# Turning batch 2's plain probabilities by transposing DMAs in a fused windowed-attention and MLP kernel

## The chip, the cores and the metric

The kernel runs on one core of a Trainium2 chip. The metric is the device time of one execution in microseconds (us), the median of several. Engines are named as in the profile: PE (TensorE), DVE (VectorE), ACT (ScalarE), POOL (GpSimd) and SP (SyncE, which here only issues DMAs).

## The reference

Eight batches of attention with 8 heads, 576 positions and 64 features per head, each followed by one layer pair of an MLP. Heads 0 to 3 see a plain window of 32 positions back; heads 4 to 7 see every fourth position of a window of 128 (a *strided* window).

```python
scores = scale * np.matmul(q, k.transpose(0, 1, 3, 2))
mask_plain = (rel >= 0) & (rel < window)                     # window = 32
mask_dil = (rel >= 0) & (rel < window * dilation) & (rel % dilation == 0)   # dilation = 4
...
attn = np.exp(scores - max)
attn = attn / (np.sum(attn, axis=-1, keepdims=True) + 1e-09)
attn_out = np.matmul(attn, v)
...
x = attn_out.transpose(0, 2, 1, 3).reshape(B * S, H * D)     # 4608 x 512
h = x @ w_in                                                 # w_in 512 x 2048
out = (h * (1.0 / (1.0 + np.exp(-h)))) @ w_out               # w_out 2048 x 512
```

## The kernel before

**Attention of one batch** is done in two halves, `z = 0` (the plain heads) and `z = 1` (the strided heads), and each half in two groups, `hi = 0` and `hi = 1`. Since only a window is seen, scores are small tiles: 32 queries by 64 keys, four of them stacked on 128 partitions. A group holds 8 or 10 such columns of 64 keys (`width`): from batch 1 on the plain half's first group has 8, so 512 elements per partition, and the three others have 10, so 640. The steps of a half are functions:

- `scores`: small matmuls on PE (L379 for `z = 0`, L391 for `z = 1`) into PSUM tiles of pool `ps`; DVE scales, masks and takes maxima (L512, L521, L528);
- `exps`: exponentials on ACT (L551 in one instruction where the maxima were already subtracted, else L560, one for each column of keys, with the sums taken along);
- `normal`: DVE divides by the sum and writes `pn` in float16 (L569 where sums are still missing, L573, L574, L576);
- the turning of `pn`, so that keys lie on partitions, into `ptT`. There are two forms. `turn` and `turned`: PE transposes 128x128 blocks, 4 or 5 for a group, into a PSUM tile of pool `ps` (L585), and a copy brings them to SBUF (L593). `turn_by_dma`: one transposing DMA from SBUF to SBUF, issued from SP (L600);
- `values`: 64 small matmuls (L627) and the rows left over (L691) into four PSUM tiles of pool `ps`;
- `finish`: four casts (L704, and L696 or L698) into `xT`, the input of the MLP.

**The MLP of one batch** is `layer1` (16 blocks, PE L717, then Silu on ACT, L725) and `layer2` (PE L782, 16 matmuls of 512 columns for a tile of 128 rows; even batches do tiles 0 to 3 of a pair of batches, odd ones tiles 4 to 8). `store` copies a tile to SBUF (L766, pool `o32` with five buffers) and issues its store from SP (L767).

**The order is written out by hand.** Instructions run on each engine in program order. While the MLP of batch `b` is issued, `plan_of(b)` puts steps of the attention of batches `b+1` and `b+2` between its pieces. `at(s, fn, ...)` puts a call at step `s`: steps 0 to 15 stand before the blocks of `layer1`, and from 16 on a step stands before each four matmuls of `layer2`, so an odd batch has steps 16 to 35. What stands at one step is issued in the order of the `at` calls. The change is in the plan of `b == 1`, in which batch 2's attention is finished and batch 3's plain scores are made.

**DMAs.** Loads are issued from POOL (`load_rows`, L134 and L141, `load_v`, L177 to L190), with a cast from float32 to float16. SP issues the stores, the transposing DMAs of whole batches of q and k (`cross`, L152 for the plain half, L158 and L159 for the strided one), and `turn_by_dma`. SP waits for the semaphores of a DMA before it issues it, and so holds up those behind it. In the plan of `b == 1` the loads of batch 4 are issued from step 17 on, batch 3's `cross` stands at step 2 and batch 4's at step 28.

**PSUM.** Pool `ps` has four tiles, pool `big` (for both layers) two. Scores of a half take three tiles of `ps`, a pair of `turn` two, `values` four.

In the plan of `b == 1`, both plain groups are normalised at step 19 and turned by PE at step 27, with their value products at step 28; the strided groups are normalised at steps 29 and 31, turned at 33, and have their products at 34. Batches 4 to 7, and the strided half of batch 3, are turned by `turn_by_dma`.

Of the kernel before, what the change touches and what calls it, by code (L numbers as in the profile page):

```python
# [29 lines left out]
def kernel(  # L30
# [764 lines left out]
    def transposes(at, b, z, step):  # L795
        for which in (1, 0):
            at(step, transpose, b, z, which, both)

    def later(at, b, z, steps, copies=(nc.vector.tensor_copy, nc.vector.tensor_copy)):

        for hi in (0, 1):
            if steps[hi] is not None:
                at(steps[hi], normal, b, z, hi)
        for hi in (0, 1):
            at(steps[2], turn, b, z, hi)
        for hi in (0, 1):
            at(steps[2], turned, b, z, hi, copies[hi])
        at(steps[3], values, b, z)
        at(steps[3], finish, b, z, copies)

    def plan_of(b):
        ev = {}

        def at(s, fn, *args):
            ev.setdefault(s, []).append((fn, args))

        def all_exps(b, z):
            for hi in (0, 1):
                at(16, exps, b, z, hi)

        if b == 0:

            at(-16, normal, 0, 1, 1)
            at(-15, shift_class, 0, dve, 1, 2)
            at(-14, normal, 0, 0, 1)
            at(-8, turn, 0, 1, 1)
            at(-8, turned, 0, 1, 1, act)
            at(-4, turn, 0, 0, 1)
            at(-4, turned, 0, 0, 1)
            at(-4, values0, 1, 1)  # L830
            at(-4, last_values, 0, 1, (1,))
            at(-4, finish0, 1, 1)
            at(-4, last_finish, 0, 1, 1)
            at(-2, values0, 0, 1)
            at(-2, last_values, 0, 0, (1,))
            at(-2, finish0, 0, 1, both)
            at(-2, last_finish, 0, 0, 1)
            at(-2, clear_short, 1, nc.vector)
            at(-2, load_v, 1)
            for c in (2, 3):  # L840
                at(-2, load_w_out, c)
            at(-2, load_qk, 2)
            transposes(at, 1, 1, 2)
            at(8, scores, 1, 1)
            for hi in (0, 1):
                at(8, shift, 1, 1, hi)
            for which in (1, 0):
                at(18, transpose, 1, 0, which, (dve, dve) if which else (act, act))
            at(20, normal, 1, 1, 0)
            at(20, scores, 1, 0)  # L850
            at(14, shift_v, 1, nc.sync.dma_start)
            at(18, load_rows, 3)
            at(18, load_v, 2)
            all_exps(1, 1)
            for hi in (0, 1):
                at(20, exps, 1, 0, hi)
            for n, z, hi in ((20, 1, 1), (26, 0, 0), (28, 0, 1)):
                at(n, normal, 1, z, hi)
            for n, z, copies in ((27, 1, (dve, dve)), (30, 0, both)):
                for hi in (0, 1):  # L860
                    at(n, turn, 1, z, hi)
                for hi in (0, 1):
                    at(n, turned, 1, z, hi, copies[hi])
                at(n + 1 + z, values, 1, z)
                at(n + 1 + z, finish, 1, z, both)
        elif b == 1:
            transposes(at, 2, 0, 3)
            transposes(at, 2, 1, 11)
            at(2, shift_v, 2, nc.sync.dma_start)
            for z in (0, 1):  # L870
                at(2, cross, 3, z)
                at(28, cross, 4, z)
            at(9, scores, 2, 0)
            for hi in (0, 1):
                at(12, shift, 2, 0, hi)
            at(17, load_v, 3)
            at(17, nc.gpsimd.tensor_copy, latch, qTs[1][:, 1, S - 1 : S])
            at(17, load_rows, 4)
            at(14, scores, 2, 1)
            all_exps(2, 0)  # L880
            all_exps(2, 1)
            for hi in (0, 1):
                at(19, normal, 2, 0, hi)
            at(21, scores, 3, 0)
            at(21, exps, 3, 0, 0)
            at(21, exps, 3, 0, 1)
            later(at, 2, 0, (None, None, 27, 28))
            later(at, 2, 1, (29, 31, 33, 34))
        else:
            if b + 2 < B:  # L890
                at(0, load_v, b + 2)
                if b + 3 < B:
                    at(0, load_rows, b + 3, (1, 0))
                if b + 3 < B:
                    at(12, cross, b + 3, 0)
                if b > 2:
                    at(12, cross, b + 2, 1)
            if b + 1 < B:
                at(1 if b == 2 else 0, shift_plain, b + 1, dve, 0, NM)
                at(12, shift_class, b + 1, dve, 0, 2)  # L900
                at(12, shift_over, b + 1, dve)
                if b == 2:
                    later(at, 3, 0, (0, 0, 4, 6))
                else:
                    at(6, values, b + 1, 0)
                    at(6, finish, b + 1, 0)
                x = {2: 13, 3: 12}.get(b, 11)
                at(x, scores, b + 1, 1)
                at(x, shift, b + 1, 1, 1)
                all_exps(b + 1, 1)  # L910
            if b + 2 < B:
                at(18 if b == 2 else 17, scores, b + 2, 0)
                for hi in (0, 1):
                    at(18, exps, b + 2, 0, hi)
            if b + 1 < B:
                for hi in (0, 1):
                    at(22 + hi, normal, b + 1, 1, hi)
                    at(22 + hi, turn_by_dma, b + 1, 1, hi)
                at(29, values, b + 1, 1)
                at(29, finish, b + 1, 1)  # L920
            if b + 2 < B:
                for hi in (0, 1):
                    at(27 + hi, normal, b + 2, 0, hi)
                    at(27 + hi, turn_by_dma, b + 2, 0, hi)

        def plan(s):
            for fn, args in ev.pop(s, ()):
                fn(*args)

        return plan  # L930
# [49 lines left out]
    for b in range(B):  # L980
        plan = plan_of(b)
        if b == 0:
            for x in range(NFF):
                plan(2 * x - NFF)
                plan(2 * x + 1 - NFF)
                layer1_part(2 * x % NFF, 2 * x // NFF, first[x] if x < 4 else None)
        else:
            for f in range(NFF):
                plan(f)
                layer1(b, f)  # L990
        if b == 0:
            layer2_first(plan)
        else:
            layer2(b, plan)
        for s in range(NFF, 3 * NFF):
            plan(s)
# [30 lines left out]
```

## Time and profile before

| | |
|---|---|
| three runs | 308.22, 307.44, 308.28 us; median 308.22 |
| the profiled execution | 307.98 us, of which the span from first to last instruction is 306.1 |
| PE | busy 294.8 us, 96% of the span; mean granted clock 0.989 |
| DVE, ACT, POOL | busy 178.2, 187.5 and 92.3 us |
| DMA, software queue (issued from POOL) | 18.88 MB in 63104 packets |
| DMA, hardware queue (issued from SP) | 19.60 MB in 41584 packets |

The profile is of one execution. The span has 40 slices of 7.65 us in the page's second part, with the busy share of each engine in tenths. "The chain" is the work that ended last, followed back from the last instruction to what released it. In a timeline a row has a start, a duration, the engine, the line, the operation, what it writes and reads, and a count; DMA rows of SP and POOL give the time of the issue, and the landing is told apart from it.

### The profile page before, as it was taken

What the parts mean: (1) busy time and instruction counts of PE and PEld (TensorE: products, weight loads), DVE (VectorE), ACT (ScalarE), POOL (GpSimd) and SP (SyncE); (2) the same over time, 40 slices, a digit from 0 to 9 for tenths busy, and PEclk for the clock granted to TensorE, in tenths of its full rate; (3) what the DMA queues carried; (4) which work ended last, traced back from release to release, by engine and by line L of the source; (5) the groups of instructions that cost most, each with busy time, mean ns of one, the idle gap of its engine ahead of it and who ended that gap; (6) DMA issues with size and microseconds to landing.
All of it is one profiled execution on the core that took longest, in us unless ns stands there. A gap on an engine that the chain in (4) does not pass through costs nothing.

```text
span 306.1 us, 10365 instructions
## 1 busy us (share of the span) xinstructions
PE 294.8 (96%) x4466; PEld 189.2 (62%) x4466; DVE 178.2 (58%) x370; ACT 187.5 (61%) x556; POOL 92.3 (30%) x139
## 2 busy tenths in 40 slices
PE   5689999999999999999999999999999999999995
PEld 2557754677555875477644775467644775477544
DVE  6896579518797738943785447842885344620011
ACT  2676677676894559945792558945793558246200
POOL 8634544962473831086007610040000000000000
PEclk9689999999999999999999999999999999999999
DMA  8999999999999999599889995494035000400022
GB/s 106 179 213 203 174 197 218 170 197 182 164 156 191 170 189 103 135 141 176 108 154 176 194 113 105 130 177 82 4 77 144 36 2 12 135 36 2 9 94 71
DMA packets 104878, 39.21 MB, mean 128 GB/s; under 512 B 79568, under 2 KB 100048, under 8 KB 104832
## 3 DMA queue, kind: packets, MB, share of 16 engines
q0 software_dynamic: 63104, 18.88, 62.6%
q1 hardware_dynamic: 41584, 19.60, 30.3%
q8 instruction: 35, 0.57, 0.8%
q14 instruction: 11, 0.09, 0.1%
q10 hardware_dynamic: 144, 0.07, 0.1%
HBM read 37.75 MB, written 9.44 MB: 154 GB/s over the span
## 4 chain that ended last, share of the span: by engine, by line
PE 87%; DMA 7%; ACT 2%; DVE 1%; issue 1%; POOL 1%; POOLq 0%; SPq 0%
PE h L717 36%; PE o L782 33%; PE o L756 5%; PE h L737 4%; DMA w_in<-in_moe_w_in_dram 4%; PE x L627 3%; DMA nat<-in_q_dram 2%; PE s L379 1%; PE s L391 1%; ACT pe L560 1%; PE t L329 1%; PE pt L585 1%; DMA ptT<-pn 1%; POOL nat L168 1%; PE xs L691 1%
## 5 line engine op out<-in xcount | busy, mean ns | idle before, releaser
L725 ACT ACTIVATE gT<-h 128x576 f16<-128x576 f32 x112 | 72.9, 651 | 77.5 <-PE h L717 77.3
L782 PE MATMUL o<-w_out,gT 128*128 128x512 f16 (+1 forms) x528 | 114.1, 373 | 0.0
L717 PE MATMUL h<-xT,w_in 128*128 128x288 f16 x896 | 113.5, 286 | 0.0
L717 PEld LDWEIGHTS <-w_in 128*128 128x128 f16 x896 | 86.4, 98 | 23.3 <-DVE xT L704 0.3
L782 PEld LDWEIGHTS <-gT 128*128 128x128 f16 x528 | 50.7, 98 | 54.9
L560 ACT ACTIVATE pe<-ms,nm 128x64 f32<-128x64 f32 x178 | 59.1, 333 | 2.8 <-DVE nm L528 2.7
L766 DVE COPY ob<-o 128x512 f32<-128x512 f32 (+1 forms) x34 | 23.1, 681 | 45.9 <-PE o L782 44.9
L512 DVE SCALAR_TENSOR_TENSOR ms<-s,mask 128x512 f32<-128x512 f32 x28 | 19.2, 686 | 35.7 <-PE s L391 24.7
L560 ACT ACTIVATION_READ_ACCUMULATOR pe<-ms,nm 128x1 f32 x178 | 33.2, 187 | 0.0
L704 DVE CAST xT<-x 128x512 f16<-128x512 f32 x26 | 16.8, 685 | 21.2 <-PE xs L691 21.2
L177 POOL DMA_DIRECT2D vw<-in_v_dram x16 | 10.1, 634 | 61.4 <-PE xs L691 59.2
L576 DVE TENSOR_TENSOR pn<-pe,r 128x640 f16<-128x640 f32 (+2 forms) x32 | 25.3, 792 | 1.1
L528 DVE TENSOR_REDUCE nm<-ms 128x10 f32<-128x640 f32 (+1 forms) x28 | 22.0, 787 | 1.0
L737 PE MATMUL h<-xT,w_in 128*128 128x256 f16 (+1 forms) x128 | 16.9, 286 | 1.6 <-issue 0.9
L134 POOL DMA_DIRECT2D nat<-in_k_dram x20 | 15.2, 764 | 6.7 <-DMA vw<-in_v_dram 6.0
L134 POOL DMA_DIRECT2D nat<-in_q_dram x20 | 14.6, 749 | 6.3 <-DMA nat<-in_k_dram 4.0
L756 PE MATMUL o<-w_out,gT 128*128 128x512 f16 x64 | 15.2, 379 | 0.2 <-issue 0.2
L737 PEld LDWEIGHTS <-w_in 128*128 128x128 f16 x128 | 11.9, 98 | 5.4 <-issue 1.9
L744 ACT ACTIVATE gT<-h 128x512 f16<-128x512 f32 (+1 forms) x16 | 10.1, 652 | 6.3 <-PE h L737 6.1
L627 PEld LDWEIGHTS <-vw 64*64 64x64 f16 x896 | 8.4, 108 | 5.2 <-issue 5.2
L766 ACT COPY ob_last<-o 128x128 f32<-128x128 f32 x1 | 0.3, 266 | 17.0 <-DVE ob_last L766 17.0
L569 DVE TENSOR_REDUCE l<-pe 128x10 f32<-128x640 f32 (+2 forms) x12 | 9.6, 801 | 1.5 <-ACT pe L551 1.4
(101 smaller groups left out, 257.7 us busy)
## 6 DMA issues: line engine op xcount, KB each, us to landing
out_dram<-ob SPq DMA_DIRECT2D x35, 256.0 KB, 2.5
vw<-in_v_dram POOLq DMA_DIRECT2D x8, 288.0 KB, 8.4
vw<-in_v_dram POOLq DMA_DIRECT2D x16, 128.0 KB, 5.6
w_in<-in_moe_w_in_dram POOLq DMA_DIRECT2D x4, 512.0 KB, 12.5
w_out<-in_moe_w_out_dram POOLq DMA_DIRECT2D x4, 512.0 KB, 11.2
nat<-in_k_dram POOLq DMA_DIRECT2D x6, 256.0 KB, 6.8
nat<-in_q_dram POOLq DMA_DIRECT2D x6, 256.0 KB, 8.2
nat<-in_k_dram POOLq DMA_DIRECT2D x20, 72.0 KB, 7.1
```

The lines of the kernel that those rows point to most:

```text
L134: nc.gpsimd.dma_start(out=f[:, 2 * (1 - which) + h // 2, 0 : ZR - 1, h % 2], in_=src[b, h].rearrange("(m p) d -> p m d", p=RT),)
L512: nc.vector.scalar_tensor_tensor(out=ms[:, 0:8].rearrange("p (n t) c -> p n (t c)", n=2), in0=s[hi].rearrange("p n t c -> p n (t c)"), sca ...
L528: nc.vector.tensor_reduce(out=nm[:, 0:w], in_=ms[:, 0:w], axis=AX.X, op=ALU.max, negate=True)
L560: nc.scalar.activation(pe[:, t, :], slot(t), AF.Exp, scale=1.0 if b else scale, bias=nm[:, t : t + 1], accum_out=l[:, t : t + 1],)
L576: nc.vector.tensor_tensor(pn[:, 0:w], a["pe", z, hi][:, 0:w], r[:, 0:w, None].broadcast_to([P, w, KB]), ALU.mult)
L627: nc.tensor.matmul(dst, w, p, start=True, stop=True)
L717: nc.tensor.matmul(h[:, half, 0:HS], w_in16[:, c, f * P : f * P + P], xT[:, c, half * HS : half * HS + HS], start=(c == 0), stop=(c == MC ...
L725: nc.scalar.activation(gT[:, f, s0 : s0 + S].rearrange("p (a c) -> p a c", a=2), h[:, :, 0:HS], AF.Silu)
L737: nc.tensor.matmul(h[:, i, 0 : c1 - c0], w_in16[:, c, (f + i) * P : (f + i + 1) * P], xT[:, c, c0:c1], start=(c == 0), stop=(c == MC - 1),)
L756: nc.tensor.matmul(o, gT[:, f, t * P : (t + 1) * P], w_out16[:, f, :], start=(f == 0), stop=(f == NFF - 1),)
L766: copy(ob, o)
L782: nc.tensor.matmul(o, gT[:, f, t * P : (t + 1) * P], w_out16[:, f, m0:m1], start=(f == 0), stop=(f == NFF - 1),)
```

## The change

For batch 2's plain half, in the plan of `b == 1`:

- each group is turned by a transposing DMA, issued from SP right behind its `normal` at step 19, in the place of nine PE transposes and two DVE copies at step 27;
- `values` and `finish` go from step 28 to step 30;
- the strided half's second `normal` goes from step 31 to step 29, beside the first, so that both now stand ahead of the plain half's `finish` in DVE's order.

`later` loses a condition that only this batch used.

```diff
     def later(at, b, z, steps, copies=(nc.vector.tensor_copy, nc.vector.tensor_copy)):
 
         for hi in (0, 1):
-            if steps[hi] is not None:
-                at(steps[hi], normal, b, z, hi)
+            at(steps[hi], normal, b, z, hi)
         for hi in (0, 1):
             at(steps[2], turn, b, z, hi)
         for hi in (0, 1):
...
             for hi in (0, 1):
                 at(19, normal, 2, 0, hi)
+                at(19, turn_by_dma, 2, 0, hi)
             at(21, scores, 3, 0)
             at(21, exps, 3, 0, 0)
             at(21, exps, 3, 0, 1)
-            later(at, 2, 0, (None, None, 27, 28))
-            later(at, 2, 1, (29, 31, 33, 34))
+            at(30, values, 2, 0)
+            at(30, finish, 2, 0)
+            later(at, 2, 1, (29, 29, 33, 34))
```

## The prediction

> **What bounds the kernel now.** I read the page's shares and slices first, then the chain of waits around batch 1's second layer, then the timelines of DVE, SP and POOL there, and last the DMAs by line.
>
> ```profile
> PE 294.8 (96%) x4466; PEld 189.2 (62%) x4466; DVE 178.2 (58%) x370; ACT 187.5 (61%) x556; POOL 92.3 (30%) x139
> PE   5689999999999999999999999999999999999995
> DMA  8999999999999999599889995494035000400022
> PE 87%; DMA 7%; ACT 2%; DVE 1%; issue 1%; POOL 1%; POOLq 0%; SPq 0%
> ```
>
> PE is full in every slice but the first few. So what leaves PE's stream comes off the end, and what PE has to wait for is added to it. The DMA engines are almost as full through 24 slices (184 us), one excepted, and batch 1's second layer (78 to 99 us, slices 11 to 13) lies in that. The chain of waits there is PE alone:
>
> ```profile
> 82.41 0.61 PE s L379 x64
> 83.02 0.08 PE ss L379 x6
> 83.10 5.29 PE o L782 x24
> 88.39 0.50 PE pt L585 x9
> 88.89 0.86 PE o L782 x4
> 89.75 0.61 PE x L627 x64
> 90.37 0.06 PE xs L691 x8
> 90.43 4.42 PE o L782 x20
> 94.85 0.56 PE pt L585 x10
> 95.41 0.86 PE o L782 x4
> ```
>
> A step of the plan is four matmuls, 0.86 us. Scores of batch 3 are step 21 (82.41), the turning of batch 2's plain pair step 27 (88.39), its value products step 28 (89.75), the strided pair's turning step 33 (94.85). No gap: PE waits for nothing here. DVE (start, us, line):
>
> ```profile
> 81.92 0.69 DVE L576 TENSOR_TENSOR pn<-pe,r 128x512 f16<-128x512 f32 x1
> 83.85 0.82 DVE L576 TENSOR_TENSOR pn<-pe,r 128x640 f16<-128x640 f32 x1
> 88.76 0.81 DVE L593 COPY ptT<-pt 128x512 f16<-128x512 f16 x2
> ```
>
> The two plain groups' `pn` are ready at 82.6 and 84.7. PE turns them 3.7 us after the second. SP's and POOL's DMAs:
>
> ```profile
> 77.35 3.86 SPq L158 DMA_TRANSPOSE strided<-nat  x1
> 81.31 2.14 SPq L159 DMA_TRANSPOSE strided<-nat  x1
> 85.31 5.53 SPq L767 DMA_DIRECT2D out_dram<-ob  x3
> 81.36 2.94 POOL L134 DMA_DIRECT2D nat<-in_k_dram  x4
> 84.26 2.96 POOL L134 DMA_DIRECT2D nat<-in_q_dram  x4
> L600 SPq DMA_TRANSPOSE ptT<-pn x18: 1199/1208/2481, 124.0 to 263.8; - x18
> DMA to landing us min/median/max: 2.4/2.6/7.9
> ```
>
> SP has issued its last transposition for batch 3 at 83.45 and idles until the store at 85.31. POOL issues batch 4's row loads from 81.36 on. The last two lines are the turnings by DMA of the later batches: 1.2 us of issue, landing 2.6 us in the median and 7.9 at worst.
>
> **The sum is made against the profiled execution**, 307.98 us (span 306.1 and 1.9 around it); the median of the three runs is 308.22, within their spread of 0.84.
>
> **Removed from PE.** Nine 128x128 transposes, 4 for the narrow group and 5 for the wide one: 0.50 us in the chain, 55 ns each. Both neighbours are matmuls at their usual pace (0.86 us for four before and after), so all 0.50 us goes. One instruction lasts 219 ns by its row, but they overlap.
>
> [...]
>
> **Removed from DVE.** Two copies PSUM to SBUF, 0.81 us in all. I cost this at nothing: PE is at matmuls meanwhile, and the only PE work behind them was step 28, which moves.
>
> **Added to SP and the DMA engines.** Two transposing DMAs, ahead of the store of tile 4. The first needs `pn` (82.6) and SP (83.45): issue at about 83.5. It takes 1.2 to 2.5 us to issue, and the second `pn` is ready at 84.7, so the second issues at 84.8 to 86.0. Behind them SP holds the stores of tiles 4, 5 and 6 and batch 4's four transpositions. The first store goes from 85.31 to 86.0 to 87.2, the others (88.87 and 90.5) hardly move. There are five store buffers, and the next tile to want tile 4's is in the following layer, at about 120 us: no one waits. Batch 4's transpositions (91.07) wait for loads; they are read by its scores at 118.44, some 17 us after they land, so a microsecond of contention is covered. If it were not, PE would wait at 118 for the excess.
>
> **Value products, moved from step 28 to step 30.** Without the turning, step 28 starts at 88.39 + 0.86 = 89.25 and step 30 at 90.97, say 91.0. That is the due time of the second DMA. Its landing is the one unknown cost. Best: 2.6 us after issue, 87.4 to 88.6, no wait. Worst: 7.9 (the turning issued at 130.12, with loads queued at the same moment), 92.7 to 93.9, a wait of 1.7 to 2.9 us. Nearest in place are the DMAs on both sides of it on the same queue: the small transposition issued at 81.31 landed after 4.7 us (2.6 for its like at 155.03, with no loads in flight), the store at 85.31 after 2.7 us, only 0.2 over the median of the stores. I take 4.3 us for a transposition between them: landing at 89.1 to 90.3, before 91.0 by 0.7 to 1.9 us. No wait, but no great margin.
>
> **DVE's order.** Both normalisings of the strided pair (2.4 us, 91.89 to 94.28 before) now stand between tile 6's copy and the plain pair's `finish`. Tile 6's copy ends at 89.9, the normalisings at 92.3 (their exponentials are done at 87.9). The products are done at 91.65, so the four casts wait 0.65 us on DVE and end at 93.8; tile 7's copy follows, done by 94.5. Who waits for that: the strided pair's turning at step 33 (now 94.35) wants the PSUM banks that the casts free at 92.9 and 93.6. Cover: 0.8 us. If it is gone, each microsecond is PE's. The two strided copies start at about 94.67, when tile 7's copy is just done, as close as before. The last casts into `xT` end at 98.0 and the next layer starts at 98.4. DVE's total falls, so I cost the reorder at nothing. From both sides: a gain is excluded because PE has no idle time there to win; a loss is at most the 0.65 us of DVE wait.
>
> **Sum.** 307.98 - 0.50 = 307.48, so 307.5 us, 0.16% less. About 0.3% (0.92 us) is what a measurement of this kernel can tell from no change; so the forecast is a small gain inside that.
>
> **Rivals.**
>
> *The second DMA lands late, and PE waits at step 30.* For it: the POOL rows above, eight loads of small packets in the same microseconds; four of the later turnings that met loads landed after 7.9, 5.6, 5.8 and 3.3 us; and SP's own 2.14 us for a transposition that elsewhere issues in 1.2. Against: the store at 85.31 passed almost freely. The change breaks even at a landing of 91.5 and is slower by over 0.92 us from 92.4. With issue at 85.5 and 7.9 us it lands at 93.4: a wait of 2.4 us, net 1.9, 309.9 us. Chance of over 0.92 us: 0.20. A landing between 91.5 and 92.4, 308.0 to 308.9: another 0.08, inside "same".
>
> [...]
>
> *The 0.50 us is refilled.* PE is then held at the same place by something else: the banks at step 33, or an output tile whose copy is late behind the normalisings. For: DVE is busy 2.4 of each 2.5 us there. Against: 0.8 us of slack at step 33, and tile 7's copy ends as early as before. 308.0 us, chance 0.08.
>
> *PE gains more than the chain shows.* If the nine transposes cost PE their full 219 ns, that is 1.97 us, and 306.0. The chain's start times (88.39 to 88.89) speak against it. Chance 0.03.
>
> **The numbers.** Forecast (no wait, or one that leaves a gain) 0.61; late by over 0.92 us 0.20; break-even or refilled 0.16; larger gain 0.03. Medians of three runs move by a few tenths of a microsecond here, so some of the forecast falls beyond 0.92 us on the faster side: 0.09 of it, with the larger gain 0.12. Slower gets 0.20 and 0.02 for the same reason from the break-even case: 0.22. The rest, 0.66, is within 0.3%. The range runs from 306.9 (the gain and a low median) to 309.2, which takes in a wait of up to 1.7 us and leaves out the worst landings.
>
> **What would show it.** Right: the chain after has no L585 between step 21 and step 33; its matmuls run on from 83.1 for nine steps to the value products at about 91.0; no idle time before L627; two L600 rows more on SP near 83.5 and 85; and the strided turning at about 94.35. Wrong: idle time of PE ahead of L627 released by the DMA `ptT<-pn`; landing of the two over 5.5 us; idle time ahead of L585 released by a cast; or scores of batch 4 that wait for `plain`.

## The result, and the profile after

The changed kernel takes 309.77 us in the median of 11 runs (308.72 to 313.23); the kernel before, run as often, 308.22 (307.44 to 309.47). The ratio is 1.0053, with a 95% interval of 1.0029 to 1.0078. So it is slower by half a per cent, where a gain of 0.16% was forecast, and outside the range. The spread has grown too. Medians here and below are of all runs; the ratios leave out runs over 1.5% above the fastest of the same kernel, of which `same_again` and `turn_first` have two each and `no_turn` one. The profiled execution took 308.80 us, with a span of 307.0.

The chain of waits after, in the same stretch (start, duration in us, what):

```profile
82.64 2.70 PE o L782 x12
...
85.45 5.21 DMA ptT<-pn
90.66 0.04 issue
90.70 0.68 PE x L627 x63
91.38 0.06 PE xs L691 x8
91.44 2.70 PE o L782 x12
94.14 0.56 PE pt L585 x10
94.70 0.86 PE o L782 x4
95.56 0.62 PE x L627 x62
96.18 0.91 issue
97.09 0.21 PE x L627 x2
```

The nine transposes are gone. The second turning lands at 90.66, and the first value products start at once. PE's rows have no idle time there: 36 matmuls from 82.64 take PE to about 90.5, so this wait is 0.2 us at most. The main loss is further down. PE stops for 0.91 us in the middle of the *strided* value products, after 62 of 64. "issue" means that the profile shows nothing that PE waited for. The change did not touch these products.

The two turnings, in SP's timeline and in the answer for L600 over 83 to 86 us:

```profile
83.64 3.02 SPq L600 DMA_TRANSPOSE ptT<-pn  x2
```

```profile
DMA to landing us min/median/max: 5.2/5.4/5.7
```

They are issued where they were expected and land after 5.7 and 5.2 us. As a measure for all runs below I take *the window*: from the first matmul of batch 1's second layer (L782) to the first of batch 2's first layer (L717), by PE's rows. It was 77.93 to 98.73 before, 20.80 us, and is 77.34 to 99.09 after, 21.75 us: 0.95 more in place of 0.50 less. From the start of the last product ahead of the gap to the start of the next is 1.10 us; the rest is in rows a little longer than before (scores 0.74 for 0.61, products 0.68 for 0.61) and in the small wait. Before and after this window the two profiles differ by what start-up and tail give.

### The profile page after: what moved, and what is told of

It is laid out like the page before. It is cut to its first block, busy times and chain, and to the rows that moved or that the text cites. A ratio compares the mean times of both kernels' runs of the same rounds, so it can differ in the third digit from the quotient of the medians.

```text
span 307.0 us, 10351 instructions
## 1 busy us (share of the span) xinstructions
PE 296.5 (97%) x4457; PEld 190.5 (62%) x4457; DVE 178.0 (58%) x368; ACT 187.3 (61%) x556; POOL 92.6 (30%) x139
## 4 chain that ended last, share of the span: by engine, by line
PE 90%; DMA 3%; DVE 2%; ACT 2%; issue 1%; POOL 1%; POOLq 0%; SPq 0%
PE h L717 36%; PE o L782 31%; PE h L737 5%; PE o L756 5%; PE x L627 3%; DMA ptT<-pn 3%; PE s L391 2%; PE s L379 2%; PE pt L585 1%; ACT pe L560 1%; PE t L329 1%; PE t L369 1%; PE xs L691 1%; DVE pn L576 1%; PE s L444 1%
## 5 line engine op out<-in xcount | busy, mean ns | idle before, releaser
L782 PE MATMUL o<-w_out,gT 128*128 128x512 f16 (+1 forms) x528 | 113.9, 373 | 0.0
L717 PE MATMUL h<-xT,w_in 128*128 128x288 f16 x896 | 113.5, 286 | 0.0
L717 PEld LDWEIGHTS <-w_in 128*128 128x128 f16 x896 | 86.4, 98 | 23.3 <-DVE xT L704 0.3
L782 PEld LDWEIGHTS <-gT 128*128 128x128 f16 x528 | 50.7, 98 | 55.1
L627 PEld LDWEIGHTS <-vw 64*64 64x64 f16 x896 | 8.7, 108 | 6.4 <-issue 6.2
L627 PE MATMUL x<-ptT,vw 64*64 64x32 f16 x896 | 10.5, 187 | 1.1 <-issue 0.9
```

The costliest lines, as they stand in the source:

```text
L627: nc.tensor.matmul(dst, w, p, start=True, stop=True)
L717: nc.tensor.matmul(h[:, half, 0:HS], w_in16[:, c, f * P : f * P + P], xT[:, c, half * HS : half * HS + HS], start=(c == 0), stop=(c == MC ...
L782: nc.tensor.matmul(o, gT[:, f, t * P : (t + 1) * P], w_out16[:, f, m0:m1], start=(f == 0), stop=(f == NFF - 1),)
```

## The experiments

Three theories. **Landing**: PE waits at step 30 for the second DMA. **Order**: DVE's normalisings ahead of the casts hold PE up. **Instruction supply**: PE is held by its own instructions.

The third comes from the page of the profile. Its instruction queue (q8) moved 35 packets and 0.57 MB, and in the trace's DMA packets each is 16 KB. PE has 4457 matmuls and as many weight loads, 8914 instructions. The 0.57 MB over these is about 64 bytes each, so a packet holds some 256 of them. Counted in weight loads and matmuls from the start of PE's stream, the gap stands at instruction 3516. The two gaps marked "issue" in the kernel before, at 21 and 48 us in start-up and batch 0, stand at 702 and 1724. Divided by 256 these leave 190 and 188, and 3516 leaves 188. So by estimate there is such a place every 256 instructions (all 45 such stops of 0.15 us or more in the 14 profiles leave 188 or 190); below I call it an *edge*, and the instructions between two edges a *block*. The previous edge, 3260, lies in the plain value products, which the change moved two steps closer.

### The change alone, without DMAs, without the turning by DMA, and DMAs alone

`same_again` is the changed kernel once more.

> The changed kernel as it is, profiled once more. In its first profile PE reached the value products of step 30 at 90.5 us, the second transposing DMA landed at 90.66, and the chain had 0.9 us of issue (PE waits for nothing that the profile shows) among the strided pair's value products at 96.2. Theory 1, landing: PE waits at step 30 for the second DMA, by an amount that differs from run to run; expected 309 to 311 us, and in the profile idle time of PE ahead of the first L627 of step 30 that equals landing minus about 90.5. Theory 2, instruction supply: PE is held by late instructions in the dense stretches of small matmuls; expected 309 to 310 us, with an issue gap of about 0.9 us near 96 us and none ahead of step 30. Theory 3, order: DVE's normalisings ahead of the casts hold PE at step 33; an idle time ahead of L585 at step 33.

310.30 us, ratio 1.0041 (1.0021 to 1.0061). Window 21.43, no idle time ahead of step 30, 0.97 us of issue after the same 62 products.

`no_turn` leaves out the turning of batch 2's plain pair:

```diff
-                at(19, turn_by_dma, 2, 0, hi)
+                at(19, no_turn, 2, 0, hi)      # products read a zeroed tile
```

> The changed kernel without the two transposing DMAs: batch 2's plain value products read a zeroed tile in place of the turned probabilities (that part of the computation is left out). PE's and DVE's orders are those of the changed kernel. Theory 1, landing: the wait is gone, 0.50 us under before, about 307.7 us, no gap at step 30. Theory 2, if PE's shorter stream alone moves the fetch into the dense stretch: the issue gap of 0.9 us stays, about 308.6 us; if the added DMA traffic delays the fetch: about 307.7. Theory 3, order: stays slower, 308.7 us or more.

309.42 us, ratio 1.0031 (1.0008 to 1.0054). Window 22.07, with 1.50 us of issue after 62 products. There is nothing to land and the gap is there, so the landing is not its cause.

`extra_dma` adds the two DMAs to the kernel before, with nobody waiting:

```diff
                 at(19, normal, 2, 0, hi)
+                at(19, turn_aside, 2, 0, hi)   # the same transposing DMA, into a spare tile
```

> The kernel before, with the same two transposing DMAs issued from SP at the same place (behind each plain normalising at step 19) into a spare tile that nobody reads; PE still turns the pair at step 27. Theory 1, landing: nobody waits for them, so no change, 308.2 us within 0.3. Theory 2 by added traffic: PE's instructions come late, 0.5 to 1 us slower, with an issue gap between 85 and 98 us. Theory 3, order: no change.

308.89 us, ratio 1.0019 (1.0003 to 1.0035). Window 20.80, no gap. The traffic alone costs at most little, and its profile doesn't show where.

`order_only` is the kernel before, turned by PE, with the new steps:

```diff
-            later(at, 2, 0, (None, None, 27, 28))
-            later(at, 2, 1, (29, 31, 33, 34))
+            later(at, 2, 0, (None, None, 27, 30))
+            later(at, 2, 1, (29, 29, 33, 34))
```

> The kernel before, still turned by PE at step 27, with the value products and finish of the plain pair at step 30 and both strided normalisings at step 29 ahead of them: the reorder alone. Theories 1 and 2: no change, 308.2 us within 0.3. Theory 3: slower by 0.4 us or more, with PE idle ahead of L585 at step 33 or ahead of the strided value products.

310.30 us, ratio 1.0049 (1.0025 to 1.0074): the whole loss, without the two DMAs. By the expectation above this is what the theory of order forecast, and not what instruction supply did. What speaks for supply is where the gap stands:

```profile
97.19 0.55 PE x L627 x53
97.74 1.46 issue
99.20 0.27 PE x L627 x10
```

The gap comes after 53 products, not 62. The nine transposes, which are still there, are nine weight loads and nine matmuls ahead of it. So it is the same instruction of the stream, 3516, and not the same piece of work. PE has no idle time ahead of the strided turning either, where a late cast would hold it.

### The normalisings or the distance

`values_late` moves only the plain products:

```diff
-            later(at, 2, 0, (None, None, 27, 28))
+            later(at, 2, 0, (None, None, 27, 30))
```

> The kernel before with one edit: the plain pair's value products and finish at step 30 in place of 28, still turned by PE, and the strided normalisings where they were, at 29 and 31. Theory 2, instruction supply: the two dense stretches of value products stand four steps apart in place of six, so the issue gap is there, 1 to 1.7 us among the strided value products, 309.3 to 310.5 us. Theory 3, order of the normalisings: no change, 308.4 us.

310.33 us, ratio 1.0044 (1.0017 to 1.0070), with 0.58 us of issue after 53 products, less than the 1 to 1.7 expected. The normalisings stand at the steps where they were, and the loss is there. But the casts of `finish` moved to step 30, so the first of the normalisings, at 29, now stands ahead of them on DVE. This run alone does not clear the order.

`no_turn_28` is `no_turn` with the plain products back at step 28; both normalisings stay at 29.

```diff
-            at(30, values, 2, 0)
-            at(30, finish, 2, 0)
+            at(28, values, 2, 0)
+            at(28, finish, 2, 0)
```

> The kernel without the two transposing DMAs (batch 2's plain value products read a zeroed tile, so that part of the computation is left out), with the plain value products and finish back at step 28; both strided normalisings at step 29. Theory 2, instruction supply, block edges: the edge in the plain products and the one in the strided products, 256 instructions on, are again some 6.6 us apart, as before (6.7 us, no gap). No gap or one under 0.3 us, and what PE no longer turns is gained: 0.3 to 0.5 us under before, 308.0 to 308.2 us. Theory 3, order of the normalisings: still slower, 309 us or more. If the gap depended on added DMA traffic or on the shorter stream alone, it would be here too.

307.73 us against 308.97, ratio 0.9967 (0.9953 to 0.9982), and all seven runs lie within 0.64 us. The chain runs through:

```profile
89.67 0.61 PE x L631 x64
...
90.35 4.42 PE o L786 x20
...
96.20 0.64 PE x L631 x64
96.84 0.14 PE xs L695 x16
```

(L631 and L786 are L627 and L782, four lines down.) The window is 78.35 to 98.65, 20.30 us: 0.50 under before, to the hundredth what the transposes were costed at. With the casts back at step 28 both normalisings stand behind them, as before, so these two runs together still can't tell the order from the distance. The runs below can: `pad_here` and `split_loads` keep the changed kernel's order, with both normalisings ahead of the casts, and have no gap here, and `turn_first` has the order of the kernel before and the longest gap of all. So order falls. What is left is how far apart the two dense stretches stand (the plain and the strided value products, 64 small matmuls in some 0.6 us each): six steps or four.

### Moving the edges

`shift_after` and `shift_before` put 64 tiny matmuls at the start of PE's stream, half a block:

```diff
     keep_busy(big.tile([P, 2, 512], F32, tag="big", name="busy")[:, 0], 4)
+    tiny = big.tile([P, 2, 512], F32, tag="big", name="tiny")
+    for _ in range(64):
+        nc.tensor.matmul(tiny[0:W, 0, 0:W], ident[:, 0:W], ident[:, 0:W], start=True, stop=True)
```

> The changed kernel with 64 tiny matmuls more at the start of PE's stream, where PE waits for the first loads anyway. Each has a weight load, so all later work lies 128 instructions further on in PE's stream, half a block of 256. Theory 2, instruction supply: the gap sits at a fixed instruction (after 62 strided products, after 53 where nine transposes stand ahead of them), the edge of a block; moved by half a block, the edge falls among the matmuls of 512 columns and the block that holds both dense stretches is gone: no issue gap between 90 and 98 us, 0.5 us under before, 307.8 to 308.2 us, unless an edge elsewhere becomes bad. Theories 1 and 3: no change against the changed kernel, 309.5 to 310.3 us.

> The kernel before with the same 64 tiny matmuls at the start: what the shift alone does. Theory 2: no gap in this place before and none after, 308.2 to 308.7 us, unless an edge elsewhere becomes bad, which the issue rows of the chain would show. Theories 1 and 3: no change, 308.4 us.

The totals miss: 316.83 us, ratio 1.0261 (1.0229 to 1.0293), and 313.97, ratio 1.0161 (1.0128 to 1.0194). In the window the expectation holds: 20.55 us and no gap for the changed kernel, 20.80 for the one before. But the other edges moved too. In the changed kernel shifted, PE waits elsewhere:

```profile
PE x L627 <- issue: 1.9, 1, 1.9
PE s L379 <- issue: 1.8, 1, 1.8
PE x L627 <- DMA ptT<-pn: 1.4, 1, 1.4
PE s L391 <- issue: 1.1, 1, 1.1
```

Its gaps stand at instructions 446, 702, 1212, 2236 and 3004, which leave 190, 190, 188, 188 and 188. The work in these places is the kernel's as it was. Ahead of batch 1's first layer the gaps make 5.6 us, where the changed kernel has 0.9, and this layer starts at 64.97 us in place of 58.30. So most of what the shift cost was lost at edges, before batch 2's attention came to its value products.

`pad_here` puts them into the changed kernel just ahead of the plain products:

```diff
+            at(27, tiny, 64)                   # 64 tiny matmuls into a PSUM tile that nobody reads
             at(30, values, 2, 0)
```

> The changed kernel with 64 tiny matmuls more (128 instructions) at step 27, into a PSUM tile that nobody reads: more work for PE, some 0.6 us by the rows of the 64 scores or products. Theory 2, block edges: the edges move half a block, out of the value products into the matmuls of 512 columns, so the issue gap at 96 us (0.9 to 1.7 us) goes; the profile has no gap between 88 and 99 us, and the time is near before, 308.3 to 308.9 us, less than the changed kernel's 310 in spite of the added work; later edges move too and could cost a few tenths. Theory 1 (landing) or 3 (order): the added work only adds, or fills a wait for the landing: 310 to 310.6 us.

312.15 us, ratio 1.0115 (1.0088 to 1.0141). The chain:

```profile
88.58 1.70 PE tiny L798 x64
...
97.77 0.64 PE x L627 x64
```

The gap is gone, as expected, and the window is 22.10, where 20.80 - 0.50 + 1.70 makes 22.00. But the tiny matmuls cost 1.70 us and not the 0.6 that I expected, and another 1.6 us is lost in batch 2's second layer, where PE waits 1.4 us for a turning of batch 3. So it shows the edge, not a cheaper kernel.

### The loads

`loads_later` was to keep batch 4's loads out of the stretch:

```diff
-            at(17, load_rows, 4)
+            at(31, load_rows, 4)
-                at(28, cross, 4, z)
+                at(34, cross, 4, z)
```

> The changed kernel with batch 4's row loads issued at step 31 in place of 17, and batch 4's cross at step 34 in place of 28, so that few loads are in flight between 83 and 93 us. Theory 2, instruction supply: PE's instructions come in blocks of 16 KB by DMA (the instruction queue of the page; 570 KB for 8932 instructions, 64 bytes each, so 256 in a block); a block comes late when loads fill the DMA engines and PE runs through 256 instructions quickly. With fewer loads the block comes in time: the issue gap of 0.9 to 1.7 us among the strided value products goes or shrinks, and the time is 307.8 to 308.3 us, under before. Theory 1, landing: the turning lands after 2.6 to 4 us and the time is the same 307.9. Theory 3, order: the gap and the 0.4% stay, 309.5 us or more.

311.94 us, ratio 1.0100 (1.0056 to 1.0144), and the edit did not do what it was for. A step did not tie POOL to PE: POOL issued the loads at 81.46 (81.36 in the kernel before). What moved was batch 4's cross, behind a store. The gap stayed (1.06 us), and 2.8 us were lost in batch 2's second layer, where PE met another gap and a late turning.

`split_loads` ties the strided loads (L141) to the end of batch 2's attention:

```diff
+    def gate():
+        nc.gpsimd.tensor_copy(latch, att(2)["xT"][:, HP - 1, S - 1 : S])
...
-            at(17, load_rows, 4)
+            at(17, load_rows, 4, (0,))
...
+            at(34, gate)
+            at(34, load_rows, 4, (1,))          # and batch 4's strided cross at step 35
```

> The changed kernel with batch 4's strided row loads held back until batch 2's attention is finished (POOL copies one element of the finished xT first) and batch 4's strided cross after the stores of the layer; the plain row loads stay. So few loads are in flight when PE's next block of instructions is fetched, between 91 and 97 us. Theory 2, with contention: the fetch starts 1 to 1.5 us after the block's edge in place of 3 to 4, the gap goes, and the time is 0.3 to 0.5 us under before, 308.0 to 308.3 us. Theory 2 without contention (a block simply takes 6 us): the gap stays, 309.5 to 310.3. A new wait at batch 4's strided scores near 145 us would show as PE idle ahead of L391.

313.71 us, ratio 1.0152 (1.0128 to 1.0176), where 308.0 to 308.3 were expected. In the window this worked: L141 at 99.93 in place of 87, and the strided products run through, though the edges are only 5.1 us apart.

```profile
97.08 0.64 PE x L627 x64
...
119.25 0.59 PE s L379 x61
119.83 2.06 issue
```

The window is 20.41, 0.39 under before. The loads then lie upon a later block: its packet starts 5.3 us after the edge ahead of it, PE stands still for 2.06 us at 119.83, and batch 3's turnings hold it for 2.5 us more in two waits.

### A version meant to be faster

`turn_first` issues the turnings ahead of batch 3's strided cross and keeps the six steps:

```diff
+            at(2, cross, 3, 0)
+            at(20, cross, 3, 1)
             for z in (0, 1):
-                at(2, cross, 3, z)
...
-            at(30, values, 2, 0)
-            at(30, finish, 2, 0)
-            later(at, 2, 1, (29, 29, 33, 34))
+            at(28, values, 2, 0)
+            at(28, finish, 2, 0)
+            later(at, 2, 1, (29, 31, 33, 34))
```

> A version meant to keep the 0.50 us: batch 2's plain pair turned by the two DMAs, but batch 3's strided cross (two transposing DMAs that are read only at 113 us) moved behind them in SP's order, from step 2 to step 20; plain value products and finish at step 28 and the strided normalisings at 29 and 31, as before. Theory 2, block edges: the two dense stretches are six steps apart again, so no issue gap near 96 us; the turnings are issued at about 82.7 and 84.8 with no other transposition ahead of them and land after 2.6 to 4.5 us, at 87.4 to 89.3, when PE wants them at 89.3: 0.50 us under before, 0.2 at worst if the second lands late; 308.0 to 308.4 us against 308.5 to 309.0. The moved cross is then in flight together with batch 4's loads; if that holds up the blocks of instructions, a gap near 96 or 105 us appears and the gain is gone. Theory 1, landing: a wait at step 28 ahead of L627, 1 us or more.

316.96 us, ratio 1.0239 (1.0200 to 1.0277): the worst case named, and more. SP's timeline, PE's waits for the turning, the chain, and the busy times by stretch:

```profile
87.05 5.01 SPq L158 DMA_TRANSPOSE strided<-nat  x1
```

```profile
PE x L627 <- DMA ptT<-pn: 0.8, 1, 0.8
```

```profile
96.88 0.62 PE x L627 x62
97.50 3.58 issue
...
101.41 3.37 PE o L782 x8
```

```profile
97.50:101.00 3.50, 0.00 (x1) 0.00 (x0) 0.69 (x1) 0.00 (x0) 0.62 (x1) 1.00 1.44 119
101.30:104.60 3.30, 3.30 (x22) 1.21 (x11) 0.95 (x3) 0.00 (x0) 3.00 (x5) 0.54 1.31 177
```

At step 28 PE waited 0.8 us for the second turning, which landed at 90.25: two steps earlier the landing is no longer covered. The cross went out together with batch 4's loads, its two DMAs took 11.5 us in the median to land, PE's next instruction packet started 8.04 us after edge 3260, and PE stood still for 3.58 us at the same edge, 3516. The column after POOL's is the granted clock: 1.00, then 0.54 behind the gap, so that eight matmuls took 3.37 us in place of 1.83.

### The edge in numbers

From the trace's DMA packets: when PE crosses edge 3260, how much later the next 16 KB packet starts, and when PE goes on at edge 3516. The last column is the time from the start of one product to the start of the next at edge 3516, where it is more than the usual hundredths.

| kernel | edge 3260 | packet starts after | on at 3516 after | step there |
|---|---|---|---|---|
| before | 89.93 | 4.22 | 6.71 | none |
| after | 90.95 | 3.82 | 6.14 | 1.10 |
| same_again | 91.12 | 3.81 | 6.18 | 1.16 |
| no_turn | 91.34 | 4.06 | 6.82 | 1.70 |
| extra_dma | 90.22 | 3.95 | 6.71 | none |
| order_only | 92.36 | 3.04 | 6.84 | 1.65 |
| values_late | 92.87 | 3.73 | 6.08 | 0.77 |
| loads_later | 91.09 | 4.07 | 6.27 | 1.25 |
| no_turn_28 | 89.94 | 2.83 | 6.70 | none |
| split_loads | 92.38 | 1.45 | 5.14 | none |
| turn_first | 90.61 | 8.04 | 10.48 | 3.77 |

Where PE was held it went on 2.2 to 2.8 us after the packet's start; in order_only 3.8, where the packet took 2.4 us and not the usual 1 (median of the 35 packets before: 1.01). In the kernel before, PE wanted the block 6.71 us after the edge, 2.49 us after the packet's start, and was not held. That lies among the 2.2 to 2.8 us, so by estimate it had 0.3 us to spare at most (0.14 with the 2.35 of `values_late`), and perhaps nothing. With the plain products moved, PE reaches edge 3260 at 13.6 us of the window and not at 12.0, and wants edge 3516 at 18.7 as before: 5 us between them, and in the profiles in which it was held there PE went on 6.1 to 6.8 us after edge 3260 (10.48 in `turn_first`). In `split_loads` the two edges are as close, the packet started after 1.45 us, and PE was not held.

The same holds for the rest of the execution. In all 14 profiles together PE has 45 stops of 0.15 us or more that are marked "issue", and each stands at an instruction that leaves 188 or 190. The kernel before has 35 such edges and 35 packets. Elsewhere a packet can start before PE crosses its edge, by 2.5 us at one place of the kernel before among matmuls of 512 columns. So the delay in the table is a measure; what asks for a packet is not shown.

64 products and their weight loads take 0.61 us, and PE stood still at edge 3516 for 0.6 to 3.6 us in the seven profiles in which it was held there.

## Why the prediction was wrong

**What bounds the kernel**: right, PE's stream. But "PE waits for nothing here" was read as a margin. By the estimate above it was one of 0.3 us at most, at an edge that no row of PE shows.

**Removed from PE, 0.50 us**: right. The window of `no_turn_28` is shorter by 0.50. That this agrees to the hundredth is partly luck: in `shift_after`, which has no gap in the window either, it is shorter by 0.25.

**The DMAs' landing**: 4.3 us was taken, and 5.7 and 5.2 were measured; over 5.5 was named as a sign of being wrong. The due time, 91.0, is by the clock of the profile before. In the profile after, PE was there at about 90.5 and the second turning landed at 90.66, so the 0.7 to 1.9 us to spare became a wait of up to 0.2 us (none in `same_again`). It is not what was lost: `order_only` has no such DMA and the same loss.

**DVE's order, at nothing**: right. In the profile after, the plain casts end at 93.36, and the strided turning runs at 94.14 with no idle time ahead of it. And with the same order `pad_here` and `split_loads` have no gap.

**Value products, moved from step 28 to step 30**: this is the step that failed. The prediction calls the landing "the one unknown cost" of it, as if PE's small matmuls cost the same wherever they stand. What the runs showed is a cost that none of the rivals named: with the two dense stretches four steps apart, PE comes to edge 3516 some 5 us after edge 3260 in place of 6.71 and goes on only 2.2 to 3.8 us after the start of the packet between them, and it loses 0.8 to 1.7 us in the six of these profiles in which it was held, against the 0.50 gained. That it waits there for this packet's instructions is my reading of these times; no row of the profile names what PE waited for.

**The rivals**: late landing had the right sign and the wrong cause and place: at step 30 PE waited 0.2 us at most, and the gap stands at step 34, where PE waits for no DMA. "The 0.50 us is refilled" supposed banks or an output tile, at 308.0 us.

**What stays open.** The medians lie some 1.3 to 1.6 us over before, and single runs up to 5.6 us. The profiled executions show gaps of 0.6 to 1.5. That the slowest runs have longer gaps of this kind fits `turn_first`, but none of those runs was profiled. Where the 0.19% of `extra_dma` goes isn't shown either; nor is it why `no_turn_28` gains 0.33% in its runs, 1.0 us, when its window gives 0.50; that the kernel before is itself held at this edge in some executions would fit its small margin, and is not shown. No version was found that computes everything and beats the kernel before: each that cleared this edge lost more elsewhere.

## What to carry to other kernels

A tensor engine that the profile shows as full (96% here) can stand close to a stop in its own instruction stream: here, by estimate from the table, within 0.3 us. Before small matmuls are moved closer together, count the instructions between dense stretches, see how long the engine takes for one block of them (6.71 us before, some 5 after), and compare that with how late the next instruction packet starts under the DMA traffic of that stretch (1.45 to 8.04 us here). And a step in a hand-written order may not hold another engine: batch 4's loads moved from step 17 to step 31 were issued by POOL at 81.46 us (81.36 before), while the copy from the finished `xT` held the strided ones until 99.93 (87.14 before).

## What the runs showed of the hardware

- An instruction packet of 16 KB started 1.45 us after the previous edge with batch 4's strided loads held back (`split_loads`), 2.8 to 4.2 us with them in flight, and 8.04 us with batch 3's strided cross beside them (`turn_first`).
- All 45 stops of PE of 0.15 us or more marked "issue" in the 14 profiles stand at instructions that leave 188 or 190 when divided by 256, weight loads counted. With 64 tiny matmuls more in the start-up the stops stood in other work, at instructions 446, 702, 1212, 2236 and 3004 (`shift_after`), and the kernels took 2.6% (changed) and 1.6% (before) longer.
- 64 matmuls of 32 columns with all 128 rows took 1.70 us, 27 ns each (`pad_here`); the 64 value products, on half the rows, take 0.61.
- After 3.58 us without a matmul, up to 101.08 us, the granted clock was 0.54 from 101.3 to 104.6 us, and 0.98 from 104.8 to 109.0 (`turn_first`).
